# One core, attention and a gated MLP: a searched instruction order replaced by another, with ScalarE's DMA queue kept to the first six head pairs

## The chip, the core and the metric

The kernel runs on one core of a Trainium2 chip. The core has five engines with a queue of instructions each: TensorE (PE, with its weight loads shown as PEld), VectorE (DVE), ScalarE (ACT), GpSimd (POOL) and SyncE (SP). An engine works through its own queue in order[...]. DMAs are issued here from SyncE and ScalarE (each has a hardware queue) and from GpSimd (a software queue). The metric is the device time of one execution in microseconds, and lower is better. Time before: 418.29 us, the median of three runs (416.84 to 419.41).

## What is computed

Attention over 8 batches, 12 heads, 448 positions and a head dimension of 64, with q and k normalised by their root mean square, followed by a two-layer MLP with a sigmoid gate over the 3584 tokens. Inputs and output are float32; the kernel computes with bfloat16 operands on TensorE.

```python
def _attn_ref(q, k, v, g_q, g_k):          # q, k, v: (8, 12, 448, 64)
    def rmsnorm(x, g):
        rms = np.sqrt(np.mean(x * x, axis=-1, keepdims=True) + 1e-06)
        return x / rms * g
    q_n, k_n = (rmsnorm(q, g_q), rmsnorm(k, g_k))
    scores = 1.0 / np.sqrt(q.shape[-1]) * np.matmul(q_n, k_n.transpose(0, 1, 3, 2))
    scores = scores - np.max(scores, axis=-1, keepdims=True)
    attn = np.exp(scores)
    attn = attn / (np.sum(attn, axis=-1, keepdims=True) + 1e-09)
    return np.matmul(attn, v)
# x = attention as (3584, 768); w_in: (768, 2048); w_out: (2048, 768)
    h = x @ w_in
    g = h * (1.0 / (1.0 + np.exp(-1.702 * h)))
    return g @ w_out
```

## The kernel before

The unit of the attention is a pair of heads of one batch: 48 pairs, numbered 0 to 47, six to a batch. The first twelve pairs (two batches) turn their operands round on TensorE, the others by DMA transposes. The MLP works by batch, and by pairs of batches in its second half, where many products are formed from sums and differences of blocks so that fewer matmuls are needed (the tasks P1 to P7 and S1 to S4 of those names).

All work is cut into tasks. A task has a kind, the indices it works on, an engine and its dependences. In this text L7,2 is the task ('L', 7, 2). The kinds that matter here:

- L i,w: the load of q (w = 0), k (1) or v (2) of pair i, 224 KB each (lines 864 and 866)
- S i: the squares of q and k of pair i, on ScalarE (875) or GpSimd (870); R i: their sums, on VectorE (884)
- Q i: the inverse root for a group of three pairs, on GpSimd (917 to 920), after Q0 i, its seed on VectorE (903, 905); for the first six pairs Q is on ScalarE (895, 896)
- N i,g: the normalised rows of q (g = 0) or k (1) in bf16 (928), and V i: v in bf16 (938 on VectorE, 941 on GpSimd)
- T i: the transposes (951 on TensorE, 963 by DMA), KQ i and K i: the scaled results put where the scores read them (955, 958, 970, 972)
- C i,h,t: the score matmuls (998); E: their exponentials on ScalarE (1006, 1008); P: the products with v (1019); O: the division (1029, 1030); B and X: the result turned into columns for the MLP (1045, 1049, 1052)
- F b,m: the first matmuls of the MLP (1225); H: tanh on ScalarE (1235); G: the gate on VectorE (1247); Y: the second matmuls (1255); U: their results copied out (1265); D: stores (1278)
- WI 0 to 3 and WO 0 to 3: the two weight matrices, 768 KB a piece as bf16, loaded and cast by GpSimd's DMAs (1194, 1200)

A constant, ORDER, holds for each engine the list of its tasks in the order in which it does them. It is the outcome of a search done before; the kernel does not search. Which engine a task stands under in ORDER also decides who does it: N, V, KQ, S and some copies have two possible engines, and a load goes through ScalarE's queue if it stands in ScalarE's list. The class _Order walks the five lists together with estimated durations and emits the tasks into the program in the sequence of their estimated starts. That walk decides three more things: which of several free PSUM banks a task takes, how many filler matmuls (line 842) TensorE does where it is expected to be idle in the first part, and whether a GpSimd instruction that follows a VectorE task marked "lock" in the early part gets a semaphore wait on it (after_lock, up to the time APART). Tile buffers are rings: raw q and k have seven slots for the first fourteen pairs and then five, so a load of a later pair waits until the pair before it in its slot has been normalised. TensorE's results of F, T, B and Y share three PSUM banks until late in the kernel.

The DMAs of the two hardware queues complete on a ring of eight semaphores in the sequence in which they were emitted, whichever queue they are on. A DMA that comes round to a semaphore waits, on the engine that issues it, for the DMA eight places before.

The loads that ScalarE issues before are these, in the sequence of its list: L0,1 L1,0 L2,0 L3,1 L0,2, then L1,2 L3,2 after Q0, L5,0 before S3, then L11,0 between H0,3 and S9, and L7,2 between E6,0 and H0,6. SyncE's list begins with L0,0 L1,1 L2,1 L3,0 L4,1 L4,0 and reaches, after L10,0 and L9,1, this stretch: L13,1 L6,2 L11,1 L12,1 L15,1 L12,0 L14,0 L13,0 L14,1 L9,2 L15,0 L8,2 L16,1. VectorE's list runs in that stretch: G0,5 O5,1 G0,6 KQ8 X5,1 K8 R11 Q0 11 G0,7 G0,8 G0,9 V7 N11,1 G0,10 G0,11 N9,0 N11,0 N9,1 O7,0. GpSimd's: Q8 N6,0 N6,1 N7,1 N7,0 N8,1 N8,0 WO0 WO1 WO2 V6 Q11 S13 N10,0 N10,1 S14 WO3 V9 Q14. TensorE's: T8 F0,7 B5,1 C7,0 F0,8 F0,9 C7,2 F0,10 F0,11 C6,2 F0,12 P7,0 F0,13 T9,0 C8,0 P6,0 F0,14 P7,1 F0,15 C8,2.

Of the kernel before, what the change touches and what calls it, by code (L numbers as in the profile page):

```python
# [12 lines left out]
ACT = mybir.ActivationFunctionType  # L13
# [11 lines left out]
BOTH, WITH_SW, SW_WITH = 0.63, 0.47, 0.69  # L25
# [3 lines left out]
APART = 45000.0  # L29


class _Order:
# [36 lines left out]
    def run(self):  # L69
# [23 lines left out]
        def share(t):  # L93
            n = len(heads())
            if n == 1:
                return 1.0
            if n == 3:
                return 0.5 if t.eng == "POOL" else 0.33
            return BOTH if not queues["sw"] else SW_WITH if t.eng == "POOL" else WITH_SW
# [44 lines left out]
        while emitted < len(self.tasks):  # L144
            best, now, got = None, NEVER, None
            for eng, names in lists.items():
                if head[eng] < len(names) and names[head[eng]].left == 0:
                    t = names[head[eng]]
# [11 lines left out]
            t, eng = best, best.eng  # L160
# [40 lines left out]
    def open(self, name, now):  # L201
# [6 lines left out]
        ('K', 0), ('R', 2, 0), ('R', 3, 0), ('KQ', 1), ('K', 1), ('N', 2, 1), ('V', 1), ('R', 4,  # L208
        0), ('KQ', 2), ('K', 2), ('O', 0, 0, 0), ('KQ', 3), ('K', 3), ('V', 2), ('O', 1, 0, 0),
        ('X', 0, 0), ('KQ', 4), ('K', 4), ('R', 5, 0), ('O', 2, 0, 0), ('V', 4), ('X', 1, 0),  # L210
        ('O', 3, 0, 0), ('N', 5, 1), ('KQ', 5), ('X', 2, 0), ('K', 5), ('O', 4, 0, 0), ('X', 3,
        0), ('V', 5), ('O', 0, 1, 0), ('R', 6, 0), ('X', 4, 0), ('O', 5, 0, 0), ('X', 5, 0),
        ('X', 0, 1), ('O', 1, 1, 0), ('R', 7, 0), ('X', 1, 1), ('R', 8, 0), ('Q0', 8), ('O', 2,
        1, 0), ('G', 0, 0), ('O', 3, 1, 0), ('G', 0, 1), ('X', 2, 1), ('R', 10, 0), ('X', 3, 1),
        ('G', 0, 2), ('KQ', 6), ('G', 0, 3), ('O', 4, 1, 0), ('K', 6), ('G', 0, 4), ('KQ', 7),
        ('K', 7), ('X', 4, 1), ('R', 9, 0), ('G', 0, 5), ('O', 5, 1, 0), ('G', 0, 6), ('KQ', 8),
        ('X', 5, 1), ('K', 8), ('R', 11, 0), ('Q0', 11), ('G', 0, 7), ('G', 0, 8), ('G', 0, 9),
        ('V', 7), ('N', 11, 1), ('G', 0, 10), ('G', 0, 11), ('N', 9, 0), ('N', 11, 0), ('N', 9,
        1), ('O', 7, None, 0), ('G', 0, 12), ('O', 6, None, 0), ('G', 0, 13), ('R', 12, 0),
        ('G', 0, 14), ('G', 0, 15), ('O', 7, None, 1), ('R', 13, 0), ('KQ', 9), ('K', 9), ('R',  # L220
        14, 0), ('Q0', 14), ('KQ', 11), ('K', 11), ('V', 8), ('O', 6, None, 1), ('KQ', 10),
        ('K', 10), ('N', 12, 1), ('O', 8, None, 0), ('X', 6, None), ('N', 13, 1), ('O', 9, None,
        1), ('R', 15, 0), ('X', 7, None), ('O', 8, None, 1), ('R', 16, 0), ('N', 14, 1), ('R',
        17, 0), ('Q0', 17), ('O', 9, None, 0), ('V', 11), ('R', 18, 0), ('V', 10), ('O', 11,
        None, 0), ('O', 11, None, 1), ('R', 19, 0), ('X', 8, None), ('O', 10, None, 0), ('X', 9,
        None), ('V', 13), ('O', 10, None, 1), ('V', 12), ('X', 10, None), ('X', 11, None),
        ('TT', 0, 1), ('TT', 0, 0), ('O', 12, None, 1), ('TT', 1, 0), ('TT', 1, 1), ('G', 1, 1),
        ('TT', 2, 0), ('O', 12, None, 0), ('G', 1, 0), ('G', 1, 2), ('G', 1, 3), ('R', 20, 0),
        ('TT', 3, 0), ('KQ', 15), ('G', 1, 4), ('G', 1, 5), ('Q0', 20), ('O', 13, None, 1),
        ('R', 21, 0), ('G', 1, 6), ('O', 13, None, 0), ('V', 15), ('G', 1, 7), ('O', 14, None,  # L230
        0), ('G', 1, 8), ('KQ', 17), ('O', 14, None, 1), ('G', 1, 10), ('O', 15, None, 1), ('G',
        1, 9), ('R', 22, 0), ('G', 1, 12), ('O', 15, None, 0), ('G', 1, 11), ('V', 16), ('TT',
        2, 1), ('G', 1, 14), ('TT', 3, 1), ('KQ', 18), ('G', 1, 13), ('G', 1, 15), ('O', 16,
        None, 0), ('S1', 0, 3), ('R', 23, 0), ('S2', 0, 3), ('U', 0, 3, 0), ('S3', 0, 3), ('O',
        16, None, 1), ('S4', 0, 3), ('X2', 0, 3), ('Q0', 23), ('V', 18), ('R', 24, 0), ('O', 17,
        None, 1), ('U', 0, 4, 1), ('N', 21, 0), ('O', 17, None, 0), ('S1', 0, 5), ('KQ', 20),
        ('U', 0, 3, 1), ('N', 23, 1), ('N', 22, 0), ('S2', 0, 5), ('S3', 0, 5), ('U', 0, 5, 0),
        ('O', 18, None, 1), ('R', 25, 0), ('O', 18, None, 0), ('R', 26, 0), ('Q0', 26), ('S4',
        0, 5), ('U', 0, 6, 1), ('O', 19, None, 0), ('U', 0, 6, 0), ('N', 24, 1), ('U', 0, 5, 1),
        ('G', 2, 0), ('O', 19, None, 1), ('G', 2, 1), ('O', 20, None, 1), ('G', 2, 2), ('G', 2,  # L240
        3), ('G', 2, 4), ('R', 27, 0), ('R', 28, 0), ('G', 2, 6), ('G', 2, 5), ('KQ', 23), ('O',
        20, None, 0), ('R', 29, 0), ('Q0', 29), ('G', 2, 7), ('G', 2, 8), ('G', 2, 9), ('KQ',
        24), ('O', 21, None, 0), ('G', 2, 11), ('G', 2, 10), ('O', 21, None, 1), ('R', 31, 0),
        ('O', 22, None, 0), ('G', 2, 13), ('V', 23), ('G', 2, 12), ('O', 22, None, 1), ('G', 2,
        14), ('G', 2, 15), ('O', 23, None, 1), ('S1', 1, 0), ('R', 30, 0), ('S2', 1, 0), ('U',
        1, 0, 0), ('O', 23, None, 0), ('R', 32, 0), ('S3', 1, 0), ('O', 24, None, 1), ('V', 25),
        ('S4', 1, 0), ('Q0', 32), ('O', 24, None, 0), ('X3', 1, 0), ('O', 25, None, 0), ('U', 1,
        1, 1), ('KQ', 28), ('N', 31, 0), ('R', 33, 0), ('U', 1, 0, 1), ('O', 25, None, 1), ('N',
        32, 1), ('G', 3, 0), ('N', 32, 0), ('G', 3, 2), ('R', 34, 0), ('G', 3, 1), ('O', 26,
        None, 1), ('R', 35, 0), ('G', 3, 4), ('O', 26, None, 0), ('Q0', 35), ('KQ', 29), ('G',  # L250
        3, 3), ('G', 3, 5), ('O', 27, None, 1), ('G', 3, 6), ('R', 37, 0), ('G', 3, 7), ('N',
        33, 0), ('G', 3, 9), ('O', 27, None, 0), ('G', 3, 8), ('G', 3, 10), ('R', 36, 0), ('G',
        3, 11), ('O', 28, None, 1), ('G', 3, 12), ('V', 29), ('R', 38, 0), ('O', 28, None, 0),
        ('Q0', 38), ('G', 3, 14), ('G', 3, 13), ('G', 3, 15), ('O', 29, None, 0), ('S1', 1, 3),
        ('S2', 1, 3), ('S3', 1, 3), ('X1', 1, 3), ('O', 29, None, 1), ('S4', 1, 3), ('N', 35,
        0), ('O', 30, None, 1), ('U', 1, 3, 0), ('S5', 1, 2), ('KQ', 33), ('X2', 1, 3), ('O',
        30, None, 0), ('X3', 1, 3), ('V', 31), ('U', 1, 4, 1), ('S1', 1, 5), ('O', 31, None, 0),
        ('U', 1, 3, 1), ('X1', 1, 5), ('R', 39, 0), ('N', 38, 0), ('S2', 1, 5), ('S3', 1, 5),
        ('U', 1, 5, 0), ('O', 31, None, 1), ('S4', 1, 5), ('O', 32, None, 1), ('R', 40, 0),
        ('R', 41, 0), ('U', 1, 6, 1), ('O', 32, None, 0), ('Q0', 41), ('V', 33), ('U', 1, 5, 1),  # L260
        ('O', 33, None, 0), ('N', 38, 1), ('N', 40, 1), ('G', 4, 0), ('G', 4, 2), ('V', 34),
        ('O', 33, None, 1), ('G', 4, 1), ('G', 4, 3), ('O', 34, None, 1), ('R', 42, 0), ('G', 4,
        4), ('G', 4, 5), ('O', 34, None, 0), ('G', 4, 6), ('V', 36), ('R', 43, 0), ('G', 4, 8),
        ('G', 4, 7), ('N', 41, 1), ('O', 35, None, 1), ('R', 44, 0), ('KQ', 38), ('G', 4, 9),
        ('G', 4, 11), ('O', 35, None, 0), ('G', 4, 12), ('G', 4, 10), ('Q0', 44), ('G', 4, 13),
        ('G', 4, 14), ('O', 36, None, 0), ('G', 4, 15), ('S1', 2, 0), ('KQ', 39), ('N', 42, 1),
        ('S2', 2, 0), ('O', 36, None, 1), ('O', 37, None, 0), ('X4', 2, 0), ('S3', 2, 0), ('S4',
        2, 0), ('O', 37, None, 1), ('U', 2, 0, 0), ('V', 39), ('O', 38, None, 0), ('R', 46, 0),
        ('U', 2, 1, 1), ('R', 45, 0), ('O', 38, None, 1), ('G', 5, 0), ('O', 39, None, 0), ('R',
        47, 0), ('Q0', 47), ('KQ', 42), ('U', 2, 0, 1), ('G', 5, 1), ('O', 39, None, 1), ('G',  # L270
        5, 2), ('O', 40, None, 0), ('G', 5, 4), ('V', 41), ('G', 5, 3), ('O', 40, None, 1),
        ('V', 42), ('G', 5, 6), ('G', 5, 5), ('KQ', 44), ('O', 41, None, 0), ('G', 5, 7), ('N',
        47, 0), ('G', 5, 8), ('O', 41, None, 1), ('G', 5, 9), ('O', 42, None, 0), ('G', 5, 11),
        ('G', 5, 10), ('G', 5, 12), ('O', 42, None, 1), ('G', 5, 13), ('O', 43, None, 0), ('N',
        47, 1), ('G', 5, 14), ('G', 5, 15), ('O', 43, None, 1), ('S1', 2, 3), ('S2', 2, 3),
# [384 lines left out]
def kernel(  # L660
# [12 lines left out]
    B, H, S, D = q.shape  # L673
# [5 lines left out]
    NP = H // 2  # L679
# [6 lines left out]
    ON_PE = NP * 2  # L686
# [466 lines left out]
    for u in units:  # L1153
        i, h = u
# [645 lines left out]
```

## Time and profile before

| what | value |
|---|---|
| three runs | 419.41, 418.29, 416.84 us, median 418.29 |
| the execution that was profiled | 417.07 us, of it 415.3 us from its first to its last instruction |
| granted TensorE clock, mean | 0.996 |
| filler matmuls (line 842) | 87, busy 13.9 us, all before 40 us |
| loads of q, k and v issued by ScalarE | 10 of 144 |
| HBM read and written | 45.61 MB and 11.01 MB |

The profile shows one execution. Its times are microseconds from the first instruction; "busy" leaves out time in which an engine only waits or issues a DMA. A line such as L1225 is a line of the kernel, and an arrow in a wait points from the instruction that waited to what released it. The chain of waits is followed back from the last instruction, at each step to what released it. The fillers count as busy TensorE, though they compute nothing that is used.

### The profile page before, as it was taken

How to read it: one execution, taken by the hardware profiler on the slowest of the kernel's cores; microseconds unless marked ns; L12 is line 12 of the kernel's file. 1: busy time of each engine (PE TensorE's matmuls, PEld its weight loads, DVE VectorE, ACT ScalarE, POOL GpSimd, SP SyncE). 2: the span in 40 equal slices, each digit the busy share in tenths (PEclk: the TensorE clock that was granted, in tenths of full speed). 3: DMA queues.
4: the chain of work that ended last, by engine and by line, in shares of the span. 5: the costliest groups of instructions: out<-in, count | busy, mean ns of one | idle time of the engine just before them, and what ended most of it. 6: DMA issues, size and time to landing. Idle time of an engine off the chain costs nothing.

```text
span 415.3 us, 10000 instructions
## 1 busy us (share of the span) xinstructions
PE 402.8 (97%) x3848; PEld 238.1 (57%) x3848; DVE 311.8 (75%) x627; ACT 300.8 (72%) x453; POOL 182.4 (44%) x274
## 2 busy tenths in 40 slices
PE   7899799999999999999999999999999999999996
PEld 5558577565555555555555555455555665555664
DVE  4988688979788968778987677877756789764642
ACT  4999585889898688877796788777888632775221
POOL 5877664681714793917452718274703200000000
PEclk9999999999999999999999999999999999999999
DMA  9999999879594778875767788458355222000354
GB/s 228 270 244 193 256 236 219 144 215 191 133 202 120 192 190 156 190 198 152 183 167 149 164 210 194 108 138 175 84 127 119 54 62 76 2 0 2 80 156 126
DMA packets 101777, 63.38 MB, mean 153 GB/s; under 512 B 55009, under 2 KB 101729, under 8 KB 101729
## 3 DMA queue, kind: packets, MB, share of 16 engines
q1 hardware_dynamic: 91360, 53.52, 54.1%
q0 software_dynamic: 7360, 6.29, 9.5%
q10 hardware_dynamic: 3008, 2.93, 2.6%
q8 instruction: 30, 0.49, 0.5%
q14 instruction: 19, 0.15, 0.2%
HBM read 45.61 MB, written 11.01 MB: 136 GB/s over the span
## 4 chain that ended last, share of the span: by engine, by line
PE 87%; DVE 4%; DMA 3%; POOL 2%; ACT 1%; issue 1%; ACTq 0%; DVEq 0%; POOLq 0%
PE w L1225 24%; PE w L1320 22%; PE o L1019 12%; PE sc L998 10%; PE b L1320 5%; PE b L1609 5%; PE w L1255 4%; PE w L1609 3%; DMA rows<-in_k_dram 3%; POOL row L928 2%; DVE row L928 1%; PE w L951 1%; DMA rows<-in_q_dram 1%; DVE ssq L884 1%; DVE obs L1030 1%
## 5 line engine op out<-in xcount | busy, mean ns | idle before, releaser
L1006 ACT ACTIVATE att<-sc 112x896 bf16<-112x896 f32 x168 | 146.6, 916 | 25.9 <-PE sc L998 25.0
L1225 PE MATMUL w<-xt,w_in_s 128*128 128x448 bf16 (+1 forms) x672 | 122.3, 328 | 0.0
L1225 PEld LDWEIGHTS <-w_in_s 128*128 128x128 bf16 x672 | 61.1, 99 | 41.9 <-issue 8.0
L1019 PEld LDWEIGHTS <-att 112*128 112x128 bf16 x1536 | 66.0, 98 | 32.1 <-issue 10.9
L928 POOL TENSOR_TENSOR row<-rows,rs 112x512 bf16<-112x512 f32 x65 | 70.6, 1108 | 8.3 <-DMA qk<-row 4.9
L1247 DVE SCALAR_TENSOR_TENSOR g<-th,w 128x448 bf16<-128x448 f32 x96 | 57.4, 613 | 16.5 <-ACT th L1235 16.4
L1235 ACT ACTIVATE th<-w 128x448 f32<-128x448 f32 x96 | 50.8, 548 | 23.1 <-PE w L1225 15.3
L1019 PE MATMUL o<-vx,att 112*128 112x65 bf16 x1280 | 63.7, 194 | 0.8 <-DVE obs L1030 0.8
L884 DVE TENSOR_REDUCE ssq<-sq 112x16 f32<-112x1024 f32 (+1 forms) x50 | 57.8, 1166 | 6.2 <-ACT sq L875 6.0
L998 PE MATMUL sc<-qk 64*128 64x448 bf16 (+1 forms) x360 | 47.8, 344 | 0.4
L941 POOL TENSOR_TENSOR vx<-rows,ones 112x512 bf16<-112x512 f32 x22 | 23.4, 1064 | 49.8 <-PE o L1019 35.9
L1030 DVE TENSOR_TENSOR obs<-o,rcp 112x256 bf16<-112x256 f32 x96 | 40.7, 424 | 3.3
L1029 DVE RECIPROCAL rcp<-o 112x4 f32<-112x4 f32 x96 | 17.0, 178 | 34.3 <-PE o L1019 34.0
L870 POOL TENSOR_TENSOR sq<-rows 112x512 f32<-112x512 f32 x29 | 32.5, 1140 | 18.2 <-DVE ssq L884 5.7
L1320 PEld LDWEIGHTS <-late 128*128 128x128 bf16 x304 | 27.4, 97 | 20.3 <-issue 3.3
L1320 PEld LDWEIGHTS <-g 128*128 128x128 bf16 x288 | 25.7, 97 | 18.1 <-issue 3.6
L917 POOL TENSOR_TENSOR t<-rs 112x48 f32<-112x48 f32 x28 | 8.0, 284 | 61.3 <-DVE rs L905 53.0
L875 ACT ACTIVATE sq<-rows 112x1024 f32<-112x1024 f32 (+1 forms) x31 | 31.4, 1020 | 4.1 <-DMA rows<-in_k_dram 4.0
L1320 PE MATMUL w<-w_out_s,g 128*128 128x384 bf16 x160 | 30.4, 326 | 0.0
L1320 PE MATMUL w<-late 128*128 128x384 bf16 x144 | 27.2, 326 | 0.7 <-DVE late L1311 0.6
L1320 PE MATMUL w<-w_out_s,late 128*128 128x384 bf16 x128 | 24.7, 326 | 0.0
L1347 ACT ACTIVATE osb<-w 128x384 f32<-128x384 f32 x25 | 12.2, 491 | 15.8 <-PE w L1320 13.3
(136 smaller groups left out, 521.0 us busy)
## 6 DMA issues: line engine op xcount, KB each, us to landing
rows<-in_k_dram SPq DMA_DIRECT2D x42, 224.0 KB, 3.8
rows<-in_q_dram SPq DMA_DIRECT2D x41, 224.0 KB, 3.7
rows<-in_v_dram SPq DMA_DIRECT2D x38, 224.0 KB, 3.7
w_in_s<-in_moe_w_in_dram POOLq DMA_DIRECT2D x4, 768.0 KB, 13.2
w_out_s<-in_moe_w_out_dram POOLq DMA_DIRECT2D x4, 768.0 KB, 14.9
out_dram<-osb SPq DMA_DIRECT2D x12, 144.0 KB, 2.8
out_dram<-osb SPq DMA_DIRECT2D x10, 168.0 KB, 2.9
out_dram<-osb SPq DMA_DIRECT2D x12, 120.0 KB, 2.5
```

Of the source, the lines that this page charges most:

```text
L870: made = [nc.gpsimd.tensor_tensor(out=sq[i % N_SQ][:SS, g], in0=raw[turn(i, N_RAW, K_RAW)][:SS, g], in1=raw[turn(i, N_RAW, K_RAW)][:SS, g] ...
L884: nc.vector.reduce_sum(out=ssq_of[g0][:SS, i - g0, part], in_=sq[i % N_SQ][:SS, part], axis=AX.X)
L928: return eng.tensor_tensor(out=row_ring[i % N_QKN][:SS, gi].rearrange("p n (h d) -> p h n d", h=2), in0=raw[turn(i, N_RAW, K_RAW)][:SS, gi ...
L998: nc.tensor.matmul(sc[:, hp, j * SH:j * SH + n], lhsT=qkw[r, k0:k0 + WIN], rhs=qk[r, 0, qs], start=True, stop=True)
L1006: nc.scalar.activation(out=att[:SS, t, :, :S], in_=sc, func=ACT.Exp)
L1019: nc.tensor.matmul(os_[u, w][:, x, :], lhsT=att_of(u)[:SS, kc, hp, qs * SS:qs * SS + WIN], rhs=vx_ring[turn(i, N_V, K_V)][:SS, hp, kc, :], ...
L1030: nc.vector.tensor_tensor(out=to[:SS, :, w, :] if h is None else to[:SS, :2].rearrange("p n h d -> p (n h) d"), in0=o[:SS, :, :D], in1=rcp ...
L1225: nc.tensor.matmul(gps[b, m][:, j * SH:j * SH + n], lhsT=w_in_s[:, ki, f * 128:(f + 1) * 128], rhs=xT[b][:, ki, lo:lo + n], start=(ki == 0 ...
L1235: nc.scalar.activation(out=th[:, :], in_=gps[b, m][:, :S], func=ACT.Tanh, scale=0.851)
L1247: nc.vector.scalar_tensor_tensor(out=g_of[b // 2][:, f:f + len(g), lo:lo + n], in0=view(ths.pop((b, m))[:, :]), scalar=1.0, in1=view(gps.p ...
L1320: nc.tensor.matmul(held[to], lhsT=lhs[:, ko, :], rhs=y[:, ko, :], start=first and ko == 0, stop=ko == NK - 1, skip_group_check=not first)
L1609: nc.tensor.matmul(joint[n, to][:, :S], lhsT=w[:, ki, n * 128:(n + 1) * 128], rhs=x[:, ki, :], start=first and ki == 0, stop=ki == KH - 1, ...
```

## The change

The list of each engine in ORDER is replaced by another one. A load may stand in ScalarE's list only for the first six pairs (it was the first twelve). Four constants of the walk are new: the shares that concurrent queues get of the DMA engines, and the time up to which GpSimd's waits for VectorE are put in.

```diff
-BOTH, WITH_SW, SW_WITH = 0.63, 0.47, 0.69
+BOTH, WITH_SW, SW_WITH = 0.63, 0.52, 0.65
...
 APART = 45000.0
+APART = 70000.0
...
             if n == 3:
-                return 0.5 if t.eng == "POOL" else 0.33
+                return 0.3 if t.eng == "POOL" else 0.45
...
-                   alt=("ACT", 430, False) if i < ON_PE else None, moves=950.0)
+                   alt=("ACT", 430, False) if i < NP else None, moves=950.0)
```

The set of tasks stays the same. Tasks with two possible engines change it in these numbers: 31 leave GpSimd and 31 others come to it, 22 leave ScalarE and 19 come, 39 leave VectorE and 40 come; SyncE has two more. TensorE's tasks are the same in another sequence, and the last 132 of its 889 stand as before. In the stretches quoted above the new lists have:

```diff
 # ScalarE
-L0,1 L1,0 L2,0 L3,1 L0,2 S0,1 S0,0 S1,0 Q0 L1,2 L3,2 Q1 S2 L5,0 S3
+L0,1 L1,0 L2,0 S0,1 S0,0 L3,1 S1,0 Q0 L0,2 L4,0 L5,0 Q1 L1,2 S2 S3
...
-H0,3 L11,0 S9 H0,4 E5,1 H0,5 E6,0 L7,2 H0,6 E6,1 S11 H0,7
+H0,3 S9 H0,4 H0,5 E6,0 H0,6 E6,1 S11 H0,7
 # SyncE
-L10,0 L9,1 L13,1 L6,2 L11,1 L12,1 L15,1 L12,0 L14,0 L13,0 L14,1 L9,2 L15,0 L8,2 L16,1 L17,1
+L10,0 L9,1 L11,0 L9,0 L13,1 L7,2 L11,1 L6,2 L12,1 L12,0 L14,0 L13,0 L15,0 L8,2 L17,0 L14,1
+L18,0 L15,1 L16,0 L9,2 L13,2 L16,1 L17,1
 # VectorE
-Q0_11 G0,7 G0,8 G0,9 V7 N11,1 G0,10 G0,11 N9,0 N11,0 N9,1 O7,0 G0,12 O6,0 G0,13 R12
+Q0_11 G0,7 G0,9 G0,8 V6 N11,1 G0,10 N10,0 N10,1 N11,0 O7,0 G0,12 G0,11 G0,13 O6,0 N9,1 N9,0 G0,14 R12
 # GpSimd
-N8,0 WO0 WO1 WO2 V6 Q11 S13 N10,0 N10,1 S14 WO3 V9 Q14 N12,0
+N8,0 WO0 WO1 WO2 V7 WO3 Q11 S14 Q14 N12,0 V9 N12,1
 # TensorE
-F0,12 P7,0 F0,13 T9,0 C8,0 P6,0 F0,14 P7,1 F0,15 C8,2 Y Y T9,1
+F0,12 P7,0 F0,13 C8,0 P6,0 F0,14 F0,15 C8,2 P7,1 T9,0 Y T9,1
```

## The prediction

> **What bounds the kernel now.** I read the busy row and the slices of the page first, then busy time by stage, then TensorE's waits, then the chain of waits through the one stage that was not full. Names such as L7,2 or H0,6 are the order lists' own; the slot of a task in the trace follows from counting a line's instructions against its list.
>
> ```profile
> PE 402.8 (97%) x3848; PEld 238.1 (57%) x3848; DVE 311.8 (75%) x627; ACT 300.8 (72%) x453; POOL 182.4 (44%) x274
> PE   7899799999999999999999999999999999999996
> ```
>
> TensorE is busy for 402.8 of 415.3 us, so all that a new order can win is 12.5 us of idle time, some of it the start and the last store, plus whatever runs at a lower clock. The stages say where it lies (columns: stage and length, PE busy, PEld, DVE, ACT, POOL, granted clock, DMA share, GB/s):
>
> ```profile
> 0.00:44.00 44.00, 39.99 (x530) 29.61 (x530) 33.83 (x80) 35.95 (x54) 32.93 (x62) 1.00 1.09 237
> 44.00:51.00 7.00, 4.08 (x52) 3.30 (x48) 3.86 (x10) 2.70 (x4) 4.28 (x5) 0.95 1.08 247
> 51.00:63.00 12.00, 11.25 (x119) 8.97 (x118) 9.89 (x17) 10.23 (x17) 7.22 (x12) 0.89 1.25 235
> 63.00:272.00 209.00, 208.91 (x2049) 117.36 (x2046) 170.22 (x342) 171.15 (x246) 112.47 (x163) 1.00 0.76 174
> ```
>
> From 63 to 272 us TensorE lacks 0.09 us: there only harm can be done. Between 44 and 51 it lacks 2.92 us in one piece, and between 51 and 63 it lacks 0.75 us and runs at 0.89 of its clock. The waits name the first:
>
> ```profile
> PE w L1045 <- DVE g L1247: 2.9, 1, 2.9
> ACT th L1235 <- DMA rows<-in_k_dram: 4.3, 1, 4.3
> ```
>
> and the chain shows what lies under it (start, length, what):
>
> ```profile
> 43.58 4.86 DMA rows<-in_k_dram
> 48.44 0.02 issue
> 48.45 0.32 ACTq L864
> ...
> 48.90 0.55 ACT th L1235
> 49.45 0.02 issue
> 49.48 0.63 DVE g L1247
> 50.11 0.04 issue
> 50.15 0.26 PE w L1045 x2
> 50.41 0.86 PE sc L998 x4
> 51.27 3.61 PE w L1225 x24
> 54.88 0.48 PE sc L998 x4
> 55.36 2.42 PE w L1225 x24
> ```
>
> ScalarE's queue holds at L864: that is L7,2, the V rows of pair 7, the only late V load that ScalarE issues. It does not need the K load (L15,1) that releases it; the built program gives both the same completion semaphore, the eighth of a ring of eight, so L7,2 cannot be issued until the load eight places before it has landed. Behind it in ScalarE's order stand H0,6 and E6,1; VectorE waits for H0,6 to make G0,6, and behind G0,6 stand KQ8, X5,1 and K8; TensorE waits for a bank. One load that nobody needs until 56 us stops three engines.
>
> **The change, part by part.**
>
> 1. *L7,2 and L11,0 leave ScalarE's queue.* In the new lists L7,2 stands on SyncE behind L13,1, L11,0 before L13,1. Nothing of ScalarE's then waits for a load's ring slot after the first six pairs. What goes: the gap, 2.92 us. And the clock: the 24 matmuls after it took 3.61 us, the same 24 at 55.36 took 2.42, so 1.19 lost; C7,0 took 0.86 against 0.48 for C7,2, so 0.38 lost; together 1.57. [...] The row shows the loss (granted clock 0.50 from 51 to 53 us), so I take 4.49[...].
>
> What is late next? S11, which needs L11,1. It landed no later than 48.4 (the chain's own landing is the next K load but one); in the new list L11,1 is still third behind L13,1, and L13,1 still waits for N6,1, which Q8 and GpSimd set at 40.5 us, unmoved. Without the stall S11 comes up at about 46.2 us (H0,6 ends 45.3, then E6,1 at 0.91). L11,1, issued at about 41.7 with the medians of 4 to 5 us, lands at 46. Cost 0 to 0.5; cover: E6,1.
>
> 2. *VectorE and GpSimd exchange tasks.* On VectorE, N9,0 N11,0 N9,1 before O7,0 become N10,0 N10,1 N11,0, and N9 moves behind O6,0; GpSimd loses N10 and S13 there. Now the chain has 2.91 us for three such casts, while GpSimd cast N10 beside them. [...] The last of the three, with GpSimd idle, took 0.68 us. In the new order GpSimd has only S14 then, which must wait for R12 anyway, so I take the row of the free case, 3 x 0.7 = 2.1 us[...]. O7,0 and with it the wait of 0.75 us at 62.6 shrink by 0.5 (bounds: 0 and 0.75). [...]
>
> 3. *T9,0 moves behind F0,15* and takes the third bank. Walking the new lists with the durations above from 47 us on: O6,0 at 59.4, N9,1 and N9,0 to 60.8, T9,0 at about 61, Y0,0,0,0 after G0,14 at 61.5. TensorE has nothing else in its order: cost 0.5 (0 to 1.5).
>
> 4. *The fourth w_out load (WO3) moves before Q11 on GpSimd.* Its issue took 0.96 us at 67.73. GpSimd stood idle 4.68 us before Q11, so the issue is hidden: V7 1.07 and WO3 0.96 after 47.2 end at 49.2, and Q0 of 11 comes at 49.3. Four such loads outstanding is not shown in the trace (at most three are). Taken as 0; if the issue held until WO0 has landed (13.3 us after 44.49), Q11 would be 8 us late. [...] Its bytes also move beside the loads of pairs 12 to 15 now; those are needed after 60 us, so that hides too, except as in rival (b).
>
> 5. *SyncE's order.* L17,0 stands before L14,1 now and waits for N10,0; L18,0 waits for N11,0, L16,0 for N9,0. Queued behind them are L14,1, L15,1, L9,2, L13,2. By step 2 N10,0 ends near 54.8, so L14,1 is issued near 55.4 instead of 45.4. The nearest row for an empty queue beside a w_out load is the one issued at 61.98, 4.8 us to landing: 60.2. S14 cannot begin before R12 (near 62.6), so it hides. L9,2 is issued near 61.4, lands near 66.5; V9 stands behind S14, Q14 and N12,0 and begins near 71. P9,1 needs it at 77.26 - 4.3 = 73. Slack 1 us, the thinnest that I found. Cost 0.
>
> 6. *The first 12 us.* ScalarE issues L4,0 before Q1 and L1,2 after it, so S2 begins near 9.8 instead of 8.84; but S3 waited for its load at 10.70 anyway, then nearly all of the order is the same. ScalarE is busy 9.2 of 10 us from 20 to 40, so a delay stays. I take +0.3 (-0.5 to +1.0). V0's load comes 1 us later, E0 too, so P0 is not held.
>
> 7. *63 to 400 us.* 31 tasks leave GpSimd and 31 come; ScalarE's and VectorE's counts move by three and one. TensorE's matmuls are the same, 87 fillers in both. The gap of 0.65 at 278.04 (the sum S2 behind N42,1, KQ and two casts) loses N42,1 from before it: -0.3. New gaps of the sort: +0.5 (0 to 4), from this stage's 0.09 and the next's 0.75.
>
> 8. *The constants.* Queue rates steer only the sequence in which tasks are written down. The reach of GpSimd's waits, 45 to 70 us, adds no wait: built with either value the new program names the same instructions and the same waits on every engine. 0.
>
> Sum: -2.92 - 1.57 - 0.5 + 0.5 + 0.3 - 0.3 + 0.5 = -4.0. The profiled execution took 417.07 us for its span of 415.3, so it would be 413.1; the median of the three runs is 418.29, which would give 414.3. I take the middle, 413.7.
>
> **Rivals.** (a) *Given back later.* VectorE is busy 170 of 209 us from 63 to 272, ScalarE 171; a matmul kept waiting there is not regained. Stalls of 0.65 us as at 278, five or six of them, eat the gain: 416 to 418. For it: nearly every list position is new. Against: the old order had none in 209 us. (b) *Slower, by SyncE's queue.* If L14,1 takes longer than 8.4 us from its issue (as four did between 45 and 48 us: 7.4 to 11.5; the longest of the kernel 13.4), S14 begins late, R14 holds VectorE, Q14 and V9 follow, and TensorE stops at P9,1. At 13.4 it is 5.0 us late, and 1.57 for the clock: +6.6 - 4.0 = +2.6, so 420.3. Against it: those four stood behind ten others. (c) *Not what it says.* ScalarE waits for L11,1 at S11 as it did at L7,2: every us that L11,1 lands after 46.2 is given back; at 49 it is 416.5.
>
> **How the numbers follow.** Forecast 0.64, spread 411.6 to 415.8 by the bounds of steps 2, 3, 6; (a) 0.20; (b) 0.09; (c) 0.07. The range to 417.8 leaves out most of (b) and the end of (a). A change of under 1% (4.2 us) can't be told from none; 414.1 is the border, so about two thirds of the forecast's chance is faster: 0.44, with 0.02 for gains that I did not see. Slower by over 1%, over 422.5, needs (a) and (b) together or step 4's hold: 0.07.
>
> **What would show it.** No ScalarE wait on a DMA between 44 and 49 us; PE without a gap over 1 us before 60 and a clock of 1.00 from 47 to 60; F0,15 near 60 us instead of 64.78; GpSimd idle between Q11 and S14; V9 done before P9,1. A gap at 72 to 74 us proves (b), many small ones behind VectorE's sums (a), a wait of the square on in_k_dram (c).

## The result, and the profile after

The changed kernel takes 413.07 us, median of four runs (410.95 to 413.40); the kernel before, measured beside it, 418.78 (416.84 to 419.41). The ratio is 0.9861, 95% interval 0.9812 to 0.9909: 1.4% faster. Executions over 1.5% above the fastest of the same kernel are left out of medians and ranges as slow; only experiment 3 had such, four of its 20, at 419.41 to 419.70 us. The changed kernel's profiled execution took 413.40 us for a span of 411.6.

First the busy time by stage of the changed kernel, in the columns of the same view of before, then TensorE's waits (total us, times, longest), then the chain of waits (start, length, what):

```profile
0.00:44.00 44.00, 39.38 (x528) 29.23 (x530) 33.00 (x80) 35.33 (x53) 33.76 (x63) 1.00 1.06 235
44.00:51.00 7.00, 6.92 (x78) 5.73 (x74) 5.87 (x12) 6.28 (x10) 5.98 (x9) 1.00 0.91 210
51.00:63.00 12.00, 12.00 (x149) 9.70 (x148) 11.53 (x21) 11.14 (x17) 2.84 (x8) 1.00 1.23 237
63.00:272.00 209.00, 207.33 (x2022) 115.78 (x2021) 165.80 (x341) 168.89 (x240) 119.97 (x173) 1.00 0.78 178
```

```profile
PE w L1256 <- DMA w_out_s<-in_moe_w_out_dram: 1.6, 1, 1.6
PE o L1020 <- ACT att L1009: 1.4, 1, 1.4
```

```profile
48.41 29.73 DMA w_out_s<-in_moe_w_out_dram
78.19 1.46 PE w L1256 x8
```

From 44 to 63 us TensorE is full (18.92 of 19 us) at the whole clock: the hold at L7,2, the gap at P6,0 and the half clock are gone. The next stage, which lacked 0.09 us before, lacks 1.67 now, nearly all of it one wait, at the second product's part Y0,0,1,2 for the last quarter of w_out. That load, WO3, took 29.73 us to land; in the kernel before it took 7.68. The wait of 1.4 us on ScalarE is at P0,0 (14.28 us), among the fillers of the start, where tasks came only 0.27 us later in all.

The same kernel measured again later (the repeat) took 411.72 us, ratio 0.9849 (0.9817 to 0.9882). Its profile has no wait on w_out. Stage rows of this second profile, then the last line on the tile w_out_s (least, median, longest us to landing) of the first and of the second profile:

```profile
63.00:272.00 209.00, 208.91 (x2040) 116.59 (x2038) 167.10 (x344) 169.89 (x243) 120.21 (x174) 1.00 0.79 179
```

```profile
DMA to landing us min/median/max: 12.5/20.2/29.7
```

```profile
DMA to landing us min/median/max: 11.4/18.3/26.6
```

WO3 landed at 75.29 us in the second profile and at 78.14 in the first; it is needed at 76.6 to 76.8. So the wait came in one of these two executions and not in the other.

The starts of single tasks on TensorE, counted against the order list, tell where the time came from (P3 is here task P of pair 3):

| task | before, us | after | after, second profile | shift, first | shift, second |
|---|---|---|---|---|---|
| P3, first half | 23.29 | 23.56 | 23.88 | +0.27 | +0.59 |
| F0,10 | 55.30 | 51.11 | 51.43 | -4.18 | -3.86 |
| C8,0 | 61.30 | 56.93 | 57.24 | -4.37 | -4.06 |
| P6,0 | 62.61 | 57.41 | 57.73 | -5.20 | -4.88 |
| P9,1 | 77.26 | 72.21 | 72.53 | -5.05 | -4.73 |
| Y0,1,1,0 | 83.77 | 80.46 | 79.04 | -3.31 | -4.73 |
| P36,1 | 274.00 | 270.71 | 269.29 | -3.29 | -4.71 |
| P38,0 | 283.50 | 279.76 | 277.81 | -3.74 | -5.69 |
| P7 2,5 | 339.19 | 335.44 | 333.49 | -3.75 | -5.70 |

Between 85 and 272 us the shift stands still: nothing is given back there.

### The profile page after: what moved, and what is told of

Read it like the earlier page. It is cut to its first block, busy times and chain, and to the rows that moved or that the text cites. A ratio compares the mean times of both kernels' runs of the same rounds, so it can differ in the third digit from the quotient of the medians.

```text
span 411.6 us, 9991 instructions
## 1 busy us (share of the span) xinstructions
PE 400.9 (97%) x3848; PEld 237.3 (58%) x3848; DVE 307.7 (75%) x628; ACT 301.0 (73%) x452; POOL 180.2 (44%) x272
## 4 chain that ended last, share of the span: by engine, by line
PE 80%; DMA 10%; POOL 4%; DVE 2%; ACT 2%; issue 1%; SPq 0%; DVEq 0%; ACTq 0%; POOLq 0%
PE w L1226 22%; PE w L1321 21%; PE o L1020 11%; PE sc L999 9%; DMA w_out_s<-in_moe_w_out_dram 7%; PE b L1321 6%; PE b L1610 4%; PE w L1610 3%; DMA rows<-in_k_dram 2%; POOL row L929 2%; PE w L1256 2%; ACT att L1009 1%; DVE ssq L885 1%; ACT sq L876 1%; POOL late L942 0%
## 5 line engine op out<-in xcount | busy, mean ns | idle before, releaser
L1007 ACT ACTIVATE att<-sc 112x896 bf16<-112x896 f32 x168 | 146.1, 917 | 27.9 <-PE sc L999 27.5
L1226 PE MATMUL w<-xt,w_in_s 128*128 128x448 bf16 (+1 forms) x672 | 120.9, 326 | 0.1
L929 POOL TENSOR_TENSOR row<-rows,rs 112x512 bf16<-112x512 f32 x66 | 71.6, 1105 | 15.6 <-DMA qk<-row 8.2
L1020 PE MATMUL o<-vx,att 112*128 112x65 bf16 x1280 | 65.3, 194 | 1.7 <-ACT att L1009 1.4
L942 POOL TENSOR_TENSOR vx<-rows,ones 112x512 bf16<-112x512 f32 x21 | 22.0, 1046 | 50.8 <-PE o L1020 46.4
L871 POOL TENSOR_TENSOR sq<-rows 112x512 f32<-112x512 f32 x27 | 30.1, 1136 | 21.6 <-DVE ssq L885 9.6
L1321 PE MATMUL w<-w_out_s,g 128*128 128x384 bf16 x160 | 31.3, 326 | 0.0
L918 POOL TENSOR_TENSOR t<-rs 112x48 f32<-112x48 f32 x28 | 8.3, 296 | 49.4 <-DVE rs L906 48.3
L1321 PE MATMUL w<-w_out_s,late 128*128 128x384 bf16 x144 | 27.4, 326 | 0.0
L1321 PE MATMUL w<-late 128*128 128x384 bf16 x128 | 24.5, 325 | 0.1
L1009 ACT ACTIVATE att<-sc 112x896 bf16<-112x896 f32 x24 | 20.8, 916 | 0.6 <-PE sc L999 0.5
```

The source lines that it names most:

```text
L871: made = [nc.gpsimd.tensor_tensor(out=sq[i % N_SQ][:SS, g], in0=raw[turn(i, N_RAW, K_RAW)][:SS, g], in1=raw[turn(i, N_RAW, K_RAW)][:SS, g] ...
L929: return eng.tensor_tensor(out=row_ring[i % N_QKN][:SS, gi].rearrange("p n (h d) -> p h n d", h=2), in0=raw[turn(i, N_RAW, K_RAW)][:SS, gi ...
L1007: nc.scalar.activation(out=att[:SS, t, :, :S], in_=sc, func=ACT.Exp)
L1020: nc.tensor.matmul(os_[u, w][:, x, :], lhsT=att_of(u)[:SS, kc, hp, qs * SS:qs * SS + WIN], rhs=vx_ring[turn(i, N_V, K_V)][:SS, hp, kc, :], ...
L1226: nc.tensor.matmul(gps[b, m][:, j * SH:j * SH + n], lhsT=w_in_s[:, ki, f * 128:(f + 1) * 128], rhs=xT[b][:, ki, lo:lo + n], start=(ki == 0 ...
L1321: nc.tensor.matmul(held[to], lhsT=lhs[:, ko, :], rhs=y[:, ko, :], start=first and ko == 0, stop=ko == NK - 1, skip_group_check=not first)
```

## The experiments

The kernel before, measured beside each, had medians of 418.38 (first four experiments), 417.84 (the next four, the repeat among them) and 418.86 us (the last four), so gains are given against the one beside them. Edits are shown as order lists.

**1. L7,2 leaves ScalarE but keeps its place among the loads.**

```diff
 # kernel before. ScalarE
-E6,0 L7,2 H0,6
+E6,0 H0,6
 # SyncE
-L8,2 L16,1
+L8,2 L7,2 L16,1
```

> The kernel before, with one task moved: the load L7,2 goes from ScalarE's list to SyncE's, behind L8,2, so that it keeps its place in the ring of completions and goes out about when it did (48 to 49 us). Theory 1 (the hold of ScalarE at L7,2 costs, and what counts is when the load goes out and who stands behind it): ScalarE's wait of 4.3 us is gone, but the load still lands near 56 us, and V7, in VectorE's order ahead of N11,1, now holds VectorE there; the gap on TensorE moves to P7,0 or F0,13 and shrinks to 1 to 3 us; 0 to 3 us faster than before. Rival 1 (leaving ScalarE's queue is all that counts): 4 to 5 us faster. Rival 2 (the gain of the change comes from the rest of the new order): 0 to 0.5 us.

Measured: 421.19 us (420.41 to 421.90), ratio 1.0065 (1.0040 to 1.0091). Slower, which no theory had said. TensorE's waits and the stage from 51 us:

```profile
PE o L1019 <- DVE vx L938: 5.5, 1, 5.5
```

```profile
51.00:63.00 12.00, 6.39 (x65) 5.08 (x62) 3.85 (x7) 6.20 (x9) 5.74 (x10) 0.85 1.25 234
```

ScalarE is free, and 44 to 51 us is full. But L7,2, issued at 49.15, landed at 60.23 (11.1 us later; from ScalarE's queue it took 7.4), and V7 needs it: VectorE stood 8.15 us before V7, from 52.1 on, and TensorE 5.5 us before P7,0. To leave ScalarE's queue is not enough. In the kernel before the hold had hidden a second lateness of the same load.

**2. L7,2 on SyncE, early.**

```diff
 # kernel before. ScalarE
-E6,0 L7,2 H0,6
+E6,0 H0,6
 # SyncE
-L13,1 L6,2
+L13,1 L7,2 L6,2
```

> The kernel before, with the same one task moved, L7,2 to SyncE, but behind L13,1, where the changed kernel has it. Theory 1: no wait of ScalarE on a load after 40 us, no gap of TensorE at B5,1, granted clock 1.00 from 47 to 56; 3.5 to 4.8 us faster than before (2.92 for the gap, 1.57 for the clock), that is about the whole gain of the change or more, since the w_out load that the changed kernel waits for by 1.6 us stays where it was. Rival 2 (the rest of the new order brings the gain): less than 1 us faster, the gap turns up at S11 or V6 instead.

Measured: 415.54 us (414.98 to 416.25), ratio 0.9932 (0.9907 to 0.9956), 2.8 us faster. L7,2 landed at 46.32. The gap at B5,1 is gone; a new one shows:

```profile
PE o L1019 <- DVE obs L1030: 1.9, 2, 1.7
```

That is 1.70 us at P6,0, which waits for O7,0 behind VectorE's casts N9,0, N11,0 and N9,1; two of these took 1.52 us each beside GpSimd's squares S13 and its cast N10,0. TensorE came 3.2 us earlier than in the kernel before (F0,13 at 56.70 instead of 59.86), O7,0 only 2.2 (59.63 instead of 61.84), since the three casts now take 3.57 us instead of 2.99. The load alone is about half of the change.

**3. The changed kernel with L7,2 back on ScalarE** (and the limit for ScalarE's loads back at the first twelve pairs).

```diff
 # changed kernel. ScalarE
-E6,0 H0,6
+E6,0 L7,2 H0,6
 # SyncE
-L13,1 L7,2 L11,1
+L13,1 L11,1
```

> The changed kernel with L7,2 put back into ScalarE's list between E6,0 and H0,6. The load eight places ahead in the ring is now L11,1, which lands near 46 to 47 us, not L15,1. Theory 1 (the price of the load on ScalarE is the landing of the load eight places ahead): ScalarE is held from about 45.7 to 46.8 at the most and S11 behind it needs the same landing anyway; 0 to 1.5 us slower than the changed kernel, TensorE's gap under 1 us. Rival 1 (a late load on ScalarE's queue costs as such): 4 us slower, back to the time before.

Measured: 415.88 us (413.04 to 418.25), ratio 0.9940 (0.9919 to 0.9960): 2.5 us faster than the kernel before, so 3.2 of the change's 5.7 us are lost, more than expected. No hold this time: its place on the ring now follows L11,1, which had landed at 45.10, and L7,2 was issued at 45.12. But it landed at 51.90, and GpSimd, which does V7 here, stood 4.60 us. Behind V7 stand WO3 and Q11; so N11,1 on VectorE came at 56.94 instead of 53.15, and

```profile
PE w L1226 <- DVE g L1248: 2.3, 1, 2.3
```

TensorE waited at F0,13. With experiments 1 and 2 this says what the load's move is worth: not the queue alone, but the landing before V7's turn. That is 47.4 us where GpSimd does V7, as here, and about 52 us where VectorE does it.

**4. The clock alone: fillers in the gap.**

```diff
 # kernel before, ahead of B5,1 on TensorE
+spare = ps_o.tile([128, NS, D + 1], FP32, tag="o", name="o")
+for _ in range(26):
+    nc.tensor.matmul(spare[:, :, :60], lhsT=ident[:, :], rhs=zeros[:, :240],
+                     start=True, stop=True)
```

> The kernel before with 26 more filler matmuls ahead of B5,1, written to the idle bank of the attention's products; they keep TensorE busy through the gap of 2.92 us and change nothing else. Theory 1 (the gap costs its length and the half clock behind it): B5,1 still begins near 50.1, the granted clock stays at 1.00 from 50 to 54, C7,0 takes 0.48 instead of 0.86 and the 24 matmuls of F0,8 and F0,9 2.4 instead of 3.6 us; 1.2 to 1.6 us faster than before. Rival (the slow matmuls there are not the clock's, or the new order's gain was the gap alone): no difference, the 24 matmuls still take 3.6 us because their banks come free late.

Measured: 417.86 us (416.96 to 420.96), ratio 0.9993 (0.9974 to 1.0012): no gain clear of noise. The stages of the profiled execution say why:

```profile
44.00:51.00 7.00, 7.00 (x91) 6.44 (x89) 3.96 (x9) 2.47 (x4) 6.41 (x7) 1.00 1.01 259
51.00:63.00 12.00, 10.67 (x113) 8.58 (x110) 9.28 (x16) 11.47 (x17) 6.77 (x12) 1.00 1.24 240
63.00:80.00 17.00, 15.94 (x173) 11.04 (x174) 13.41 (x30) 8.76 (x13) 8.15 (x14) 0.90 0.95 174
```

From 44 to 63 us the clock stays at 1.00, and from F0,7 to F0,11 TensorE wins 1.56 us on the kernel before, the 1.57 that the half clock costs. Then it waits 0.56 us at F0,13, 0.61 at T9,0 and 0.99 at P6,0. F0,13 waits for a gate of VectorE, and VectorE had stood before V7:

```profile
DVE vx L938 <- DMA rows<-in_v_dram: 1.6, 1, 1.6
```

That is L7,2 itself, which landed at 58.53. The loss of the half clock was real, and covered: the same load's landing, by way of VectorE, was next. After these waits the clock halves at 65 us, but that belongs to this execution, the slowest of the 14 and one of two at a mean clock of 0.992. Ten of the 14 ran at a mean clock of 0.998 or more, with a median of 417.76 us; the kernel before ran at 0.996 or less in all its 35. So the clock alone is worth at most about 0.6 us (an estimate, 417.76 against 418.38), not 1.57.

**5. What the late weight load costs.** The changed kernel again (the repeat), and beside it one with other work of TensorE in front of the task that waits:

```diff
 # changed kernel. TensorE
-Y0,0,1,1 Y0,0,1,2 Y0,0,1,3 P9,0 (0,1) C11,2 P9,0 (2) Y0,1,1,0 P9,0 (3)
+Y0,0,1,1 C11,2 P9,0 (0,1,2,3) Y0,1,1,0 Y0,0,1,2 Y0,0,1,3
```

> The changed kernel itself, as the measure for the three runs beside it: 413 us median (0.3% either way), with the 1.58 us wait of TensorE at the second product's third part (Y0,0,1,2) at about 76.6 us in its trace.

> The changed kernel with C11,2, the four sums of P9,0 and the part Y0,1,1,0 of the next output tile placed on TensorE before Y0,0,1,2, the first to read the last quarter of w_out (WO3). Theory (the wait at 76.6 us is paid to the end, and is one of order alone): 2.4 us of other work fill it, the gap goes from 1.58 to below 0.3 us, and the time falls by 1.2 to 1.6 us, to about 411.6. Rival (given back: the work that was moved ahead is missing later, at the exponentials of pair 11 behind S18,0 on ScalarE, or at the sum P11): the gap at Y0,0,1,2 goes but 0.5 to 1.5 us of new gap shows between 80 and 95 us, and the time falls by less than 0.6.

Measured: 411.72 us for the changed kernel (410.67 to 413.89), 412.59 with the other order (411.37 to 413.58; ratio to before 0.9857, 0.9826 to 0.9889). No gain. Both expectations failed on one point, that the wait is there every time. In the profile of the other order WO3 landed at 76.65 and nothing waits for it, but C11,2 now waits 0.41 us.

**6. WO3 issued late, as before.**

```diff
 # changed kernel. GpSimd
-V7 WO3 Q11 S14 Q14
+V7 Q11 S14 WO3 Q14
```

> The changed kernel with the load of WO3 back behind S14 in GpSimd's list, where it stood in the kernel before: issued at about 63.9 instead of 48.4 us. Theory (the software queue serves its loads one after another, WO3 starts only when WO2 has landed at 69.9, and the eleven loads of SyncE issued from 55 to 64 us slow it): WO3 lands again at 77 to 79 us, the wait stays between 1 and 2.5 us, the time within 0.8 us of the changed kernel's. Rival 1 (the move to the front is what made it late, a load among four shares its lanes): it lands about 8 us after its issue, as before, at 72, the wait goes, 1.5 us faster. Rival 2 (late issue costs in full): it lands after 80, and the kernel is slower by 2 us or more.

Measured: 411.96 us (411.57 to 414.23), ratio 0.9864 (0.9830 to 0.9898), no different from the repeat beside it. The wait of 1 to 2.5 us that was expected did not come. WO3 was issued at 65.25 instead of 48.71 and landed at 77.78 instead of 75.29: 16.5 us of issue time, 2.5 us of landing. Of the 2.5, 1.1 is this execution's later start (P3 at 24.98 instead of 23.88). Most of it stands in WO2's landing already, at 70.40 in this run and at 68.21 in the repeat: WO3 came 7.4 and 7.1 us after it. The two loads behaved as if served one after the other, whenever WO3 was issued. Step 4's worry about four loads outstanding was unfounded (in the changed kernel WO3's issue, at 48.41, took 0.94 us); but an earlier issue does not bring an earlier landing in proportion.

**7 and 8. VectorE's casts, with the load's move and without it.**

```diff
 # 7: experiment 2's kernel; 8: the kernel before. VectorE
-G0,11 N9,0 N11,0 N9,1 O7,0 G0,12 O6,0 G0,13
+G0,11 N11,0 O7,0 G0,12 O6,0 N9,0 N9,1 G0,13
 # TensorE
-F0,13 T9,0 C8,0
+F0,13 C8,0
...
-F0,15 C8,2 Y0,0,0,0
+F0,15 C8,2 T9,0 Y0,0,0,0
```

> The kernel before with the two edits on which the theory rests: L7,2 (values of pair 7) on SyncE's queue behind L13,1, and on VectorE the casts N9,0 and N9,1 behind O6,0, with T9,0 on TensorE behind C8,2; nothing else. Theory (the load's move frees ScalarE, but VectorE's casts before O7,0 hand 1.7 us of that back at P6,0): the 1.70 us gap at P6,0 goes to below 0.4, and the time falls from the 415.5 of the load's move alone to about 413.8 (1.4 to 2.0 us less). Rival (the gap moves to T9,0 or Y0,0,0,0 because the casts of pair 9 come too late, and the next wait is WO3's or pair 9's values'): 0.5 us less or none, gaps of 1 us or more at 60 to 78 us.

> The kernel before with VectorE's casts N9,0 and N9,1 behind O6,0 and T9,0 behind C8,2 on TensorE, and L7,2 left where it was on ScalarE's queue: the other edit of the pair alone. Theory (ScalarE's hold of 3 us at L7,2 stays, so the exponentials and E8 stay late; the casts only remove the gap of 0.75 us at P6,0 and lay bare what stood behind it): 0 to 0.8 us faster, the gap of 2.9 us at B5,1 stays. If the two edits add up, the load's move is worth 2.8, both together 3.9 (measured), so this one 1.1. Rival (the casts are the whole of the second half and the load only helps through them): 2 us or more faster.

Measured: both edits 413.95 us (413.31 to 415.78), ratio 0.9900 (0.9869 to 0.9931), 3.9 faster; the casts alone 417.77 (416.61 to 418.79), ratio 0.9977 (0.9963 to 0.9992), 1.1 faster. With the load's 2.8 they add up: 2.8 + 1.1 = 3.9. In the kernel with both, the 1.70 at P6,0 has become 0.6 (below 0.4 was expected), and Y0,0,0,0, behind T9,0 in its new place, waits 0.5:

```profile
PE o L1019 <- DVE obs L1030: 0.9, 2, 0.6
...
PE w L1255 <- DVE g L1247: 0.5, 1, 0.5
```

Two moves make 3.9 of the 6.1 us. As to the rest: counted from P3, the kernel with both falls 1.5 us behind the repeat by P9,1, and another 1.0 between P36,1 and P38,0, where it still has the 0.65 us gap of before.

**9 and 10. The order spliced at 61 us.** One kernel has the new order up to TensorE's C8,2 (ScalarE's H0,15, VectorE's G0,15, GpSimd's Q11) and the old one for what is left; the other is the reverse.

```diff
 # 9, the seam. VectorE (new, up to G0,15)      GpSimd (new up to Q11, then old)
+G0,10 N10,0 N10,1 N11,0 O7,0 ... G0,15         V7 WO3 Q11 | S13 S14 V9 Q14
 # 10, the seam. VectorE (old, then new)        GpSimd (old up to Q11, then new)
+... O6,0 G0,13 R12 G0,14 G0,15 | N10,0 N10,1   WO2 V6 Q11 | WO3 S14 Q14 N12,0 V9
```

> The changed kernel's order on every engine up to about 61 us (TensorE through C8,2, ScalarE through the last gate of the first product, VectorE through G0,15, GpSimd through Q11 with WO3 in front of it, SyncE through L15,1), and from there on the remaining tasks in the order and on the engines of the kernel before. Theory (the gain is made before 61 us; the rest of the new order is worth only the 0.65 us gap at 278 us and some 0.3 besides): 4.5 to 5.5 us faster than before, 0.7 to 1.3 slower than the changed kernel. Rival (the new order after 61 us carries the load: the old order can't use the earlier start, since its transfers and VectorE's tasks keep their old times): less than 3.5 us faster than before, with new gaps between 65 and 100 us.

> The reverse: the order of the kernel before up to the same point (SyncE through L13,0), then the remaining tasks as the changed kernel has them. Theory: only the late parts of the change are left, 0.5 to 1.3 us faster than before, with the 2.9 us gap at B5,1 still there and no 0.65 us gap at 276 us. Rival: 2.5 us or more faster. If the two splices add up, their gains sum to the 6.1 us of the whole change (measured in the last call).

Measured: new head 415.74 us (413.80 to 416.23), ratio 0.9925 (0.9904 to 0.9946), 3.1 faster where 4.5 to 5.5 were expected, so the rival's forecast came (under 3.5, with a new gap between 65 and 100 us); new tail 419.64 (418.14 to 420.65), ratio 1.0020 (1.0007 to 1.0033), 0.8 slower where a gain was expected. The two sum to 2.3 us, not to 6.1. The halves fit each other, and each seam breaks one fit, so these runs do not measure "head" and "tail" by themselves. What they do show is two delays.

In the new head GpSimd does S13 at 55.6 us, which the changed kernel gives to ScalarE, and VectorE's casts N10,0, N10,1, N11,0 stand beside it. VectorE's timeline, changed kernel first, then the splice (start, length, form):

```profile
54.29 1.89 DVE L929 TENSOR_TENSOR row<-rows,rs 112x512 bf16<-112x512 f32 x3
```

```profile
55.90 3.32 DVE L929 TENSOR_TENSOR row<-rows,rs 112x512 bf16<-112x512 f32 x3
```

The same three casts take 1.89 us with GpSimd idle and 3.32 beside its squares, with 1.27 and 1.52 for the two that overlap. TensorE waits 0.74 us at P6,0 for it. It waits another 0.86 at P9,1: V9, which stands ahead of Q14 in the old tail, had to wait for L9,2 (landed at 70.59), and a cast and O on VectorE came late behind Q14.

In the new tail N10,0 comes only at 67.4 us, since the old head has left it to GpSimd and the new tail leaves it to VectorE. Its chain of waits:

```profile
67.39 0.61 DVE row L929
...
68.06 0.31 SPq L867
...
68.41 4.28 DMA rows<-in_k_dram
...
72.76 1.05 POOL sq L871
...
73.83 1.22 DVE ssq L885
```

SyncE holds L17,0 until N10,0 is done; behind it stands L14,1, for which GpSimd's S14 waits, then VectorE's sum, then Q14 and V9. TensorE lost 0.84 us at P8,0 and 0.63 at P9,1. This is the prediction's rival (b), come about by a late cast instead of a slow load.

The same hold shows something else. Between 48.3 and 68.06 us SyncE issues no load, and the quarters of w_out land 3.86, 3.91 and 3.86 us apart, though WO3 is issued 9 us after WO2. In the kernel before, where SyncE issues none from 47.4 to 61.98 us, WO1 and WO2 come 4.11 and 4.01 us after the quarter ahead. In the changed kernel, with eleven loads of SyncE issued from 55 to 64 us, the quarters land 5.58, 7.09 and 8.29 us apart.

**11. Fillers in experiment 8's kernel.** Edit: that of experiment 4 added to that of experiment 8.

> The third run's base with the casts moved (N9,0 and N9,1 behind O6,0, T9,0 behind C8,2 in the kernel before), and 26 small products of TensorE into an idle o bank before B5,1, which fill the gap at 44 to 47 us without doing any of the work, so that the clock is not lowered. Theory (the half clock's 1.57 us is real but was covered by VectorE's casts before O7,0; with the casts gone from there it is laid bare): 1.0 to 1.6 us faster than the same kernel without the fillers, granted clock 1.00 from 44 to 63 us. Rival (VectorE is still last at P7,0 or P6,0, by V7 or the gates behind ScalarE's hold): within 0.5 us of the kernel without the fillers.

Measured: 417.89 us (417.30 to 419.11), ratio 0.9990 (0.9976 to 1.0003), against 417.77 without the fillers. The rival is right. Again the wait moved on: VectorE stood 1.67 us before V7 for L7,2, and TensorE waited 0.57 us at F0,13 and 0.77 at P6,0. The profile of the kernel without fillers shows no half clock, although its gap at B5,1 is 2.69 us, but it is one of only two of 14 executions at a clock of 1.000. The other twelve ran at 0.990 to 0.996; with the fillers, ten of 14 ran at 0.998 or more. So in most executions there was a lost clock to win back, and winning it back did not change the time.

None of the variants beats the changed kernel.

## Why the prediction was right, step by step

The forecast was 413.7 us; 413.07 was measured, and 411.72 in the repeat. Against the medians beside them that is -5.7 and -6.1 us where -4.6 was forecast. The terms, from the table of starts:

| step | predicted, us | first profile | second profile |
|---|---|---|---|
| 1, hold and half clock | -4.49 | -4.45 | -4.45 |
| 2, casts before O7,0 | -0.5 | -0.82 | -0.82 |
| 3, T9,0 (and what moves around P7,1) | +0.5 | -0.05 | -0.05 |
| 4, WO3 | 0 | +1.74 | 0 |
| 6, the start | +0.3 | +0.27 | +0.59 |
| 7, 63 us to the end | +0.2 | -0.45 | -0.98 |
| sum | -4.0 | -3.8 | -5.7 |

Step 1 is P3 to F0,10, behind the 24 matmuls that ran at half clock; step 2 is C8,0 to P6,0; step 3 is F0,10 to C8,0 and P6,0 to P9,1; step 4 is P9,1 to Y0,1,1,0; step 7 is what follows. That the first sum comes so near is in part luck: the missed 1.74 us of step 4 is set off by what steps 2, 3 and 7 brought over their terms.

*Step 1.* The size was right and the reason incomplete. The half clock of the trace (0.50 from 51 to 53 us) belonged in the sum: the shift of 4.45 us contains it. But the prediction took the gap and the clock as sums on TensorE's path. By experiments 4 and 11 the clock alone is worth 0.6 us at most, since VectorE, which waits for the landing of the same load, comes next. Experiment 1 shows that to free ScalarE is worth nothing while L7,2 lands at 60.23; in experiment 3 its landing at 51.90 loses more than half of the gain. The gain needs the landing before V7's turn, on GpSimd at 47.4 us, which the prediction only touched ("nobody needs until 56 us"). It held since the new place gives it: L7,2 landed at 45.7.

*Step 2.* Mis-sized by 0.3 us, and it carries more than its term says: without it the load's move is worth 2.8 us. The row of the free case, 0.68 us, was the right one to take: GpSimd is busy 2.84 of 12 us in that stretch, none of it beside these casts, and they took 0.68 to 0.69 us each. The splice shows the other case in the same place: 1.52 us beside GpSimd's squares.

*Step 3.* T9,0 cost nothing: Y0,0,0,0 did not wait. In the kernel with only the two moves it did, 0.5 us: there G0,14, which Y0,0,0,0 reads, stands behind R12 (1.2 us) on VectorE, and in the new order it stands ahead of R12.

*Step 4.* The failed term: "those are needed after 60 us, so that hides too". The prediction asked whether the loads wait for WO3's bytes and not whether WO3 waits for theirs. WO3 follows WO2 (landed at 69.85 us) beside eleven loads of SyncE issued from 55 to 64 us; two of these, L11,2 and L13,2, were issued at 77.35 and 85.53 before. And TensorE needs WO3 5 us earlier than before. That SyncE's loads stretch it is shown by the new tail, where they are held back and the quarters land 3.9 us apart instead of 5.6 to 8.3. Slack went from 6.5 us (75.40 against 81.88) to between +1.5 and -1.58.

*Step 5.* The issues came as predicted, L14,1 at 55.40 us, V9 at 70.94, done 0.23 us before P9,1 began. The landings came 2.4 and 3.4 us later than predicted (L14,1 at 62.62, L9,2 at 69.94) and just fitted: S14 read L14,1 at 62.87. The new tail shows what stood behind that slack.

*Step 6.* The size was right (+0.27 and +0.59), but "P0 is not held" was not: TensorE stands 1.4 us before P0,0 for ScalarE's E in the first profile and 0.4 in the second. It began there at 14.28 and 14.60 us all the same, and at 14.78 before.

*Step 7.* The one gap of 0.65 us at 278 went wholly, and few new gaps came; predicted was half of that gap and 0.5 of new ones. The rest is the base: the profiled execution of before (417.07) was 0.8 to 1.8 us faster than the medians measured later, so steps summed against it are to be set against those medians.

Rival (a) did not come, (c) did not (L11,1 landed at 46.82, S11 began at 46.95). *Step 8* is not tested by a run.

Open: which of the other moves before P9,1 bring the 1.5 us that the pair of moves lacks; whether WO3's spread from one execution to the next has a cause inside the kernel; and what L11,0's move alone does.

## What to carry to other kernels

A hold on one queue is worth removing only as far as the next thing that the same lateness delays: look for what stands behind it on the other engines (here VectorE's casts, then the load's own landing) and move these in the same step. Where the order moves earlier, ask of every large transfer that keeps its time how much slack it has left, in the direction "what slows it" as well as "what it slows". Before believing half a per cent, profile the same kernel twice.

## What was not expected of the hardware

The half clock came in pieces of 3.4 us (6.8, twice that, in experiment 1) and did not follow the length of the gap. These are TensorE's stage rows (busy, clock, DMA share, GB/s) of the new-tail splice after a gap of 2.55 us, of experiment 8 after a gap of 2.69 us, and of experiment 6 after one of 1.94 us in the start:

```profile
52.00:52.50 0.50, 0.50 (x5) 0.54 1.21 250
52.50:55.00 2.50, 2.50 (x16) 0.50 1.19 277
55.00:55.50 0.50, 0.50 (x5) 0.54 1.22 269
```

```profile
52.00:55.50 3.50, 3.50 (x35) 1.00 1.20 261
```

```profile
16.00:16.50 0.50, 0.50 (x10) 0.88 1.13 231
16.50:19.50 3.00, 3.00 (x22) 0.50 1.14 238
19.50:20.00 0.50, 0.50 (x6) 0.71 1.15 238
```

A gap of 2.55 us is followed by 3.4 us at half clock (52.04 to 55.46), one of 2.69 by none, one of 1.94 by 3.4 us (16.38 to 19.79), beginning 1.6 us after its end. In the kernel before, 3.4 us at half clock (50.30 to 53.71) begin 0.15 us after the end of the gap of 2.92; in experiment 2 none follow the gap of 1.70.

So in these traces a gap of 1.70 to 2.92 us was followed by no half clock or by 3.4 us of it (1.57 us lost in the kernel before). The length of the gap does not tell which, and what does is not shown. Executions of one kernel differ in their clock, and in their time with it: in experiment 6 the four at a clock of 0.999 or 1.000 took 411.57 to 412.22 us, the two at 0.995 and 0.996 took 414.15 and 414.23.
